# Output products on float16 parts scaled by row, and attention buffers in another order

## The chip, the cores and the metric

The kernel runs on one core of a Trainium2 chip. The time is the device time of one execution in microseconds (us). The engines are TensorE (PE, with its weight loads shown as PEld), VectorE (DVE), ScalarE (ACT), GpSimd (POOL) and SyncE (SP), which issues the DMA transfers. Each engine works through its own list of instructions in order; semaphores make it wait for the others.

## What is computed

Three parts follow each other: attention over 8 batches and 8 heads with 576 tokens of 64 values and a block-causal mask; a soft mixture of 8 experts with 4 slots each; and a feed-forward layer with a squared ReLU. Its weights `w_in` and `w_out` come as float64.

```python
def _attn_ref(q, k, v):                      # [8, 8, 576, 64] each
    ...
    scores = scale * np.matmul(q, k.transpose(0, 1, 3, 2))
    block_i = pos[:, None] // block
    block_j = pos[None, :] // block
    scores = np.where(block_i >= block_j, scores, -1000000000.0)
    scores = scores - np.max(scores, axis=-1, keepdims=True)
    attn = np.exp(scores)
    attn = attn / (np.sum(attn, axis=-1, keepdims=True) + 1e-09)
    return np.matmul(attn, v).astype(np.float32)

def _moe_ref(x, phi, w1, w2):                # x [4608, 512], phi [512, 32]
    logits = x @ phi
    d = np.exp(logits - logits.max(0, keepdims=True))
    d /= d.sum(0, keepdims=True) + 1e-09
    slot_input = (d.T @ x).reshape(E, S_per_e, D)
    for e in range(E):
        h = np.maximum(slot_input[e] @ w1[e], 0.0)
        slot_out[e] = h @ w2[e]
    ...
    c = np.exp(logits - logits.max(1, keepdims=True))
    c /= c.sum(1, keepdims=True) + 1e-09
    return (c @ slot_out).astype(np.float32)

def _moe2_ref(x, w_in, w_out, s, b):         # w_in [512, 2048], w_out [2048, 512]
    h = x @ w_in
    r = np.maximum(h, 0.0)
    g = s * (r * r) + b
    return (g @ w_out).astype(np.float32)
```

## The kernel before

The 4608 tokens are 36 tiles of 128. Attention runs as 32 pairs of heads whose operations are put in order by a planner from due times; in it the float16 products `pv` of probabilities and values (L405 to L407) take the probabilities and values as a high and a low part. Its buffers lie in the pools `earlyp` and `latep`. Weights come in as `wseq` lists them: four pairs of tiles of `w_in`, then eight tiles `wo_0` to `wo_7` of `w_out`, then 16 pieces of w1 and 16 of w2 (1 MB each, in two halves). Twelve tiles have a place from the start (`NPRE`); the four last of `w_out` go to the pool `wlate`, the expert weights to `NPOST` places of the pool `wpost` and to those that become empty (`advance`, `used`). These pools lie where attention's buffers were, so a load waits until the buffers under it are free. SP issues the loads in this order.

After attention comes the middle. A float64 value is turned into float32 by `from_f64` (L604 to L620): DVE cuts exponent (`cve`) and mantissa (`cvm`) out of the high word, ACT turns the low word into a float (`cvf`, L611) and shifts the exponent (L612), DVE puts the parts together (L614, L615), and `finish` follows, one function a step. For `w_out`, `split_wo` has three: the value (DVE, L690), its high part rounded to fp32r (ACT, L696) and its low part, the rest (DVE, L251), both into one tile `wo_is`. Two conversions run at a time; `convert` takes one step of each in turn, so the instructions of a pair of tiles alternate. Between them stand the expert products on PE: `expert1` (L787) into hp, then `hs` and `hTz` (L801 to L806), `expert2` (L815) into so, 32 pieces in all. The same rounds take up six chains `combine` (L760 to L777) for the combine weights: a maximum (DVE), a difference (POOL), an exponential (ACT, L767), sum and reciprocal (DVE), and the parts `cs` (POOL, ACT).

Then the slots stage: `slot_rows` copies so into `sos` (ACT, L861), transposes it (L864) and copies it to `soT` (DVE, L865). `slots` multiplies it by the converted `w_in` (L872, L879) into `mst`, 2048 columns, which holds a high part in its upper and a low part in its lower rows. `ctrans` transposes three token tiles of `cs` into `ct` (L626).

The output stage has 12 groups g of three token tiles, and in each 16 steps f of 128 rows of `w_out`. A step's h product is mst by ct (PE, L902, 384 columns), r its ReLU (ACT, L904), g is s·r² (DVE, L910), rh the rounded g + b (ACT, L916), rl the rest (DVE, L918). Four steps later (`LAG`) nine o products of 512 columns follow: for each token tile rh by high, rh by low and rl by high (L930 to L932). After 16 steps `stage_e` copies the three results and sends them out. All matrix operands here are fp32r. The order of this stage and of the middle is the order of the code.

## Time and profile before

| | us |
|---|---|
| three runs | 1007.74, 1008.96, 1010.03 |
| median | 1008.96 |
| the profiled execution | 1010.36 |
| its span in the profile | 1008.6 |

| engine | busy us | share of the span |
|---|---|---|
| PE | 902.7 | 89% |
| DVE | 696.9 | 69% |
| ACT | 564.7 | 56% |
| POOL | 283.7 | 28% |

The rows further down are of two views. A window row gives a stretch of the span, its length, for PE, PEld, DVE, ACT and POOL the busy time with the count of instructions, then the TensorE clock that was granted (1.00 is 2.4 GHz, 0.50 is 1.2 GHz), the share of the DMA engines that was busy and GB/s. A timeline row gives the start of an instruction, how long it is shown, engine, line, operation, out<-in with the partitions, shape and type; "x2" stands for so many alike in a row, and brackets for the idle time before it and what ended that. Matrix instructions overlap in the engine, so their pitch is the difference of two starts, not the duration shown.

### The profile page before, as it was taken

To read this page: it belongs to the slowest core of one execution; us is meant where nothing else is said; L and a number is where in the kernel's file an instruction comes from. 1 tells how busy PE (TensorE), PEld (TensorE's weight loads), DVE (VectorE), ACT (ScalarE), POOL (GpSimd) and SP (SyncE) were. 2 spreads that over 40 slices of the span, in tenths; PEclk is the share of its full clock that TensorE was granted. 3 is DMA by queue.
4 is the path that set the end of the run, shared out by engine and by line. 5 is a ranking of instruction groups with operands and counts; after the bars stand their busy time and mean duration, and the time that the engine had idled before them with its cause. 6 is when DMAs were issued, how large, how long until landed. Compare 5 with 4: busy or idle time off the path is not lost.

```text
span 1008.6 us, 20366 instructions
## 1 busy us (share of the span) xinstructions
PE 902.7 (89%) x8032; PEld 689.5 (68%) x8032; DVE 696.9 (69%) x1236; ACT 564.7 (56%) x974; POOL 283.7 (28%) x223
## 2 busy tenths in 40 slices
PE   3999989988999899955765999999999999999998
PEld 2777767766777777732111588888888888888886
DVE  5798979878989788768995555555555555555553
ACT  2677767767777677743453544444444444444442
POOL 6576647655666566720003000000000000000000
PEclk9999999989999999975978899999999999999999
DMA  4535445344434443085994000000000100010001
GB/s 113 129 85 121 121 104 130 79 106 119 111 98 123 104 101 101 4 333 203 403 385 176 1 1 32 32 26 8 32 32 1 31 32 1 32 32 6 26 32 31
DMA packets 150927, 91.73 MB, mean 91 GB/s; under 512 B 127472, under 2 KB 127792, under 8 KB 150832
## 3 DMA queue, kind: packets, MB, share of 16 engines
q1 hardware_dynamic: 150832, 90.44, 30.1%
q8 instruction: 63, 1.03, 0.4%
q14 instruction: 32, 0.26, 0.1%
HBM read 80.81 MB, written 9.44 MB: 89 GB/s over the span
## 4 chain that ended last, share of the span: by engine, by line
PE 60%; DVE 23%; ACT 7%; issue 3%; POOL 3%; DMA 2%; SPq 1%; DVEq 0%; ACTq 0%; POOLq 0%
PE o L932 13%; PE o L931 13%; PE o L930 13%; PE s L367 5%; DVE vl L345 3%; PE h L902 3%; DVE mm L281 3%; ACT pc L372 3%; PE tp L257 3%; DVE cvf L614 2%; DMA mr<-mT 2%; PE s L292 2%; DVE cve L615 2%; ACT ph L244 2%; PE pv L405 2%
## 5 line engine op out<-in xcount | busy, mean ns | idle before, releaser
L251 POOL TENSOR_TENSOR pl<-pc,ph 128x896 f16<-128x896 f32 (+1 forms) x128 | 232.2, 1815 | 153.3 <-ACT ph L244 79.3
L910 DVE SCALAR_TENSOR_TENSOR g<-r,s_sb 128x384 f32<-128x384 f32 x192 | 118.6, 618 | 156.9 <-ACT r L904 155.6
L904 ACT ACTIVATE r<-h 128x384 f32<-128x384 f32 x192 | 94.1, 491 | 197.8 <-PE h L902 197.8
L372 ACT ACTIVATE pc<-s 128x896 f32<-128x896 f32 (+1 forms) x128 | 110.6, 864 | 80.6 <-PE s L367 52.6
L918 DVE SCALAR_TENSOR_TENSOR rl<-g,b_sb,rh 128x384 fp32r<-128x384 f32 x192 | 117.7, 613 | 6.9 <-ACT rh L916 6.9
L916 ACT ACTIVATE rh<-g,b_sb 128x384 fp32r<-128x384 f32 x192 | 116.9, 609 | 0.6 <-DVE g L910 0.6
L244 ACT CAST ph<-pc 128x896 f16<-128x896 f32 (+1 forms) x128 | 113.4, 886 | 4.1
L281 DVE TENSOR_REDUCE mm<-s 128x2 f32<-128x1024 f32 (+3 forms) x128 | 101.8, 817 | 9.0 <-PE s L292 8.9
L405 PE MATMUL pv<-vh,ph 128*128 128x65 f16 x960 | 102.8, 196 | 1.7 <-DVE xt L421 1.5
L405 PEld LDWEIGHTS <-ph 128*128 128x128 f16 x960 | 86.8, 98 | 23.9 <-issue 6.7
L407 PE MATMUL pv<-vh,pl 128*128 128x65 f16 x960 | 101.3, 194 | 1.4 <-POOL pl L251 1.4
L406 PE MATMUL pv<-vl,ph 128*128 128x64 f16 x960 | 101.6, 193 | 0.0
L407 PEld LDWEIGHTS <-pl 128*128 128x128 f16 x960 | 88.9, 98 | 1.6 <-POOL pl L251 1.5
L406 PEld LDWEIGHTS <-ph 128*128 128x128 f16 x960 | 88.8, 99 | 0.0
L251 DVE TENSOR_TENSOR kql<-tp,kq 128x512 fp32r<-128x512 f32 (+1 forms) x96 | 57.5, 599 | 30.2 <-ACT kq L273 29.2
L257 PE MATMUL tp<-idF,rqk 128*128 128x128 f32 x320 | 58.5, 301 | 21.1 <-DVE kql L251 8.6
L367 PE MATMUL s<-mr,neg 64*128 64x128 f32 (+3 forms) x384 | 68.0, 321 | 7.4 <-DMA mr<-mT 7.0
L367 PE MATMUL s<-kq 64*128 64x128 f32 (+3 forms) x384 | 71.2, 367 | 0.7
L292 PE MATMUL s<-kq 64*128 64x64 f32 (+4 forms) x384 | 55.9, 337 | 16.8 <-DVE me L281 11.2
L902 PE MATMUL h<-ct,mst 128*128 128x384 f32 x192 | 65.5, 342 | 1.4 <-ACT r L904 1.4
L345 DVE SCALAR_TENSOR_TENSOR vl<-rv,al,vh 128x640 f16<-128x640 f32 x32 | 63.9, 1996 | 0.9 <-POOL vh L342 0.9
L273 ACT CAST kq<-tp 128x512 fp32r<-128x512 f32 (+1 forms) x96 | 48.5, 505 | 27.2 <-PE tp L257 27.0
(241 smaller groups left out, 2060.1 us busy)
## 6 DMA issues: line engine op xcount, KB each, us to landing
w2h<-in_moe_w_dram SPq DMA_DIRECT2D x34, 512.0 KB
w<-in_moe_w_dram SPq DMA_DIRECT2D x30, 512.0 KB
rqk<-in_k_dram SPq DMA_DIRECT2D x64, 128.0 KB
rqk<-in_q_dram SPq DMA_DIRECT2D x64, 128.0 KB
rv<-in_v_dram SPq DMA_DIRECT2D x64, 128.0 KB
wi<-in_moe_w_in_dram SPq DMA_DIRECT2D x8, 1024.0 KB
wo<-in_moe_w_out_dram SPq DMA_DIRECT2D x8, 1024.0 KB
out_dram<-ob SPq DMA_DIRECT2D x32, 256.0 KB
```

Source lines behind the costliest of these rows:

```text
L244: ACT.copy(o, i)
L251: eng.tensor_tensor(out=o, in0=i, in1=h, op=ALU.subtract)
L281: DVE.tensor_reduce(out=o, in_=i, axis=AX, op=ALU.max)
L367: PE.matmul(ps[:, h, o:o + c1 - c0], a[r], b[r], start=(n == 0), stop=(n == 3))
L372: ACT.activation(out=pc[:, :, 0:w], in_=st.pop(("ps", p, c))[:, :, 0:w], func=AF.Exp, scale=scale)
L405: PE.matmul(o, a, vh[:, 2 * sl + h, 0:65], start=(c == 0 and n == 0), stop=False)
L406: PE.matmul(o[:, 0:64], a, vl[:, 2 * sl + h, :], start=False, stop=False)
L407: PE.matmul(o, l, vh[:, 2 * sl + h, 0:65], start=False, stop=(c == 3 and n == len(UNIT[c]) - 1))
L910: DVE.scalar_tensor_tensor(out=g0, in0=r, scalar=s_sb, in1=r, op0=ALU.mult, op1=ALU.mult)
L930: PE.matmul(o, rh[:, 128 * i:128 * i + 128], hl[f][0], start=(f == 0), stop=False)
L931: PE.matmul(o, rh[:, 128 * i:128 * i + 128], hl[f][1], start=False, stop=False)
L932: PE.matmul(o, rl[:, 128 * i:128 * i + 128], hl[f][0], start=False, stop=(f == 15))
```

## The change

**Output products.** `rh`, `rl` and the two parts of `w_out` become float16. So that they keep to float16's range, each row of `w_out` (a partition and a half of a tile) is multiplied by a power of two: a new step `power` of `split_wo` stands between value and high. ACT sums the magnitudes of a row of 512 (`wsum`, with the accumulating output), DVE turns the sum's exponent into an inverse power (`wpow`), and ACT scales that by 2^13. High is then written by two scaled copies of 512 on ACT, low by two operations of 512 on DVE. Two tiles `wo` now share one home, so every second conversion frees a place for an expert weight. The g side takes the inverse: s and b become `sk` and `bk`, a column for each f, which follow from a bound over `mst`, s, b and `wsum`. That takes 16 transposes of mst, a maximum over them, some small operations on 128 x 16, a product on PE to bring the maximum over the partitions, and more small ones; they stand between the last `mst` and the first g. `stage_e` multiplies by `mu`, which undoes the scale.

**Buffers.** Attention's buffers are allocated in the order in which the last pairs of heads free them; `wlate` is opened ahead of `e1` and handed out from its other end; `cvm` has one buffer instead of two, and `NPOST` is 4.

```diff
@@ -18,7 +18,7 @@
 PSUM = bass.MemoryType.PSUM
 
 NPRE = 12
-NPOST = 3
+NPOST = 4
 
 SLOT = {
     "ld_k": -28.8, "ld_q": -28.6, "ld_v": -18.0,
@@ -121,6 +121,9 @@
     m896 = const.tile([128, 1], F32, name="m896")
+    eps = const.tile([128, 1], F32, name="eps")
+    wsum = const.tile([128, 16], F32, name="wsum")
+    wpow = const.tile([128, 16], F32, name="wpow")
@@ -137,6 +140,7 @@
     POOL.memset(m896, -896.0 * 2.0 ** 23)
+    POOL.memset(eps, 2.0 ** -100)
@@ -145,13 +149,18 @@
     RQK = [earlyp.tile([128, 2, 5, 128], F32, name=f"rqk_{i}") for i in range(2)]
-    RV = [earlyp.tile([128, 5, 128], F32, name=f"rv_{i}") for i in range(2)]
-
-    KQ = [earlyp.tile([128, 2, 640], F32R, name=f"kq_{i}") for i in range(3)]
-    KQL = [earlyp.tile([128, 2, 640], F32R, name=f"kql_{i}") for i in range(3)]
-
-    MR = [earlyp.tile([128, 640], F32R, name=f"mr_{i}") for i in range(2)]
+    KQ, KQL, MR = [None] * 3, [None] * 3, [None] * 2
+    for p in (NP - 3, NP - 2, NP - 1):
+        KQ[p % 3] = earlyp.tile([128, 2, 640], F32R, name=f"kq_{p % 3}")
+        KQL[p % 3] = earlyp.tile([128, 2, 640], F32R, name=f"kql_{p % 3}")
+        if p == NP - 3:
+            RV = [earlyp.tile([128, 5, 128], F32, name=f"rv_{i}") for i in range(2)]
+        else:
+            MR[p % 2] = earlyp.tile([128, 640], F32R, name=f"mr_{p % 2}")
@@ -602,7 +611,7 @@
-        m = pool.tile([128, n], I32, tag="cvm", name="cvm")
+        m = pool.tile([128, n], I32, tag="cvm", name="cvm", bufs=1)
         e = pool.tile([128, n], I32, tag="cve", name="cve")
         f = pool.tile([128, n], F32, tag="cvf", name="cvf")
@@ -642,8 +651,8 @@
+    wlate = wholes(ctx, "wlate", 16 - NPRE, reuse_waits="tile")
     e1 = later(ctx, "e1", 1)
-    wlate = wholes(ctx, "wlate", 16 - NPRE, reuse_waits="tile")
     P["cv"] = later(ph2, "cv", 2)
     wpost = places(ph2, "wpost", NPOST, reuse_waits="tile")
@@ -674,7 +683,7 @@
 
             key = toload.pop(0)
-            home[key] = wlate.pop() if key[0] == "wo" else empty.pop()
+            home[key] = wlate.pop(0) if key[0] == "wo" else empty.pop()
             load_w(key, home[key])
 
     def used(key):
@@ -686,22 +695,39 @@
     def split_wo(i):
         def value(u, s):
             DVE.tensor_tensor(out=u, in0=u, in1=s, op=ALU.mult)
 
+        def power(u, s):
+            for h in range(2):
+                ACT.activation(out=s[:, 512 * h:512 * h + 512], in_=u[:, 512 * h:512 * h + 512], func=AF.Abs, bias=eps,
+                               accum_out=wsum[:, 2 * i + h:2 * i + h + 1])
+            DVE.tensor_scalar(out=wpow[:, 2 * i:2 * i + 2].bitcast(I32), in0=wsum[:, 2 * i:2 * i + 2].bitcast(I32),
+                              scalar1=0x7F800000, scalar2=0x7F800000, op0=ALU.bitwise_and, op1=ALU.bitwise_xor)
+            ACT.mul(wpow[:, 2 * i:2 * i + 2], wpow[:, 2 * i:2 * i + 2], 2.0 ** 13)
         def high(u, s):
-            t = home["wo", i].tile([128, 2048], F32R, tag="w", name=f"wo_{i}s")
+            if i % 2 == 0:
+                st["wos", i // 2] = home["wo", i].tile([128, 2, 2, 2, 512], F16, tag="w", name=f"wo_{i}s")
+            t = st["wos", i // 2][:, i % 2]
             for h in range(2):
-                hl[2 * i + h] = t[:, 512 * h:512 * h + 512], t[:, 1024 + 512 * h:1536 + 512 * h]
-            ACT.copy(t[:, 0:1024], u)
-            st["wos", i] = t
+                hl[2 * i + h] = t[:, h, 0], t[:, h, 1]
+                ACT.activation(out=t[:, h, 0], in_=u[:, 512 * h:512 * h + 512], func=AF.Copy,
+                               scale=wpow[:, 2 * i + h:2 * i + h + 1])
 
         def low(u, s):
-            t = st.pop(("wos", i))
-            lo(DVE, t[:, 1024:2048], u, t[:, 0:1024].bitcast(F32))
+            for h in range(2):
+                DVE.scalar_tensor_tensor(out=hl[2 * i + h][1], in0=u[:, 512 * h:512 * h + 512],
+                                         scalar=wpow[:, 2 * i + h:2 * i + h + 1], in1=hl[2 * i + h][0],
+                                         op0=ALU.mult, op1=ALU.subtract)
             ready.update((2 * i, 2 * i + 1))
-
-        return from_f64(wt["wo", i], P["cv"], [value, high, low])
+            if i % 2:
+                empty.append(split(home["wo", i], i))
+                advance()
+        return from_f64(wt["wo", i], P["cv"], [value, power, high, low])
 
     def conv_in(i):
 
@@ -882,6 +908,9 @@
+        sb_abs = e1.tile([128, 2], F32, name="sb_abs")
+        ACT.activation(out=sb_abs[:, 0:1], in_=s_sb, func=AF.Abs)
+        ACT.activation(out=sb_abs[:, 1:2], in_=b_sb, func=AF.Abs)
         slot_rows()
         ctrans(0, pm, "n")
         gens = [slots(i) for i in range(8)]
@@ -890,6 +919,34 @@
                 next(gens[i])
             if i >= 2:
                 next(gens[i - 2], None)
+        mt = pm.tile([128, 512], F32, tag="m", name="m")
+        for f in range(16):
+            PE.transpose(mt[:, 32 * f:32 * f + 32].bitcast(F32R), mst[0:32, 128 * f:128 * f + 128], idR[0:32, 0:32])
+        def small(name, n=16):
+            return e1.tile([128, n], F32, name=name)
+        mm, bound, gpow, sk, bk, rs_, mu = (small(n) for n in ("mmax", "bound", "gpow", "sk", "bk", "rscale", "mu"))
+        DVE.tensor_reduce(out=mm, in_=mt.rearrange("p (f n) -> p f n", n=32), axis=AX, op=ALU.max)
+        DVE.tensor_tensor(out=mm, in0=mm, in1=mm, op=ALU.mult)
+        DVE.tensor_scalar(out=mm, in0=mm, scalar1=sb_abs[:, 0:1], scalar2=sb_abs[:, 1:2], op0=ALU.mult, op1=ALU.add)
+        DVE.tensor_scalar(out=gpow.bitcast(I32), in0=wsum.bitcast(I32), scalar1=0x7F800000, scalar2=None, op0=ALU.bitwise_and)
+        DVE.tensor_tensor(out=bound, in0=mm, in1=gpow, op=ALU.mult)
+        DVE.tensor_reduce(out=mu[:, 0:1], in_=bound, axis=AX, op=ALU.max)
+        gp = pm.tile([128, 512], F32, tag="n", name="n")
+        PE.matmul(gp[:, 0:128], mu[:, 0:1].to_broadcast([128, 128]), idF, start=True, stop=True)
+        DVE.tensor_reduce(out=mu[:, 1:2], in_=gp[:, 0:128], axis=AX, op=ALU.max)
+        DVE.tensor_scalar(out=mu[:, 1:2], in0=mu[:, 1:2], scalar1=2.0 ** -60, scalar2=None, op0=ALU.max)
+        DVE.tensor_scalar(out=mu[:, 2:3].bitcast(I32), in0=mu[:, 1:2].bitcast(I32), scalar1=0x7F800000, scalar2=0x7F800000,
+                          op0=ALU.bitwise_and, op1=ALU.bitwise_xor)
+        DVE.tensor_scalar(out=rs_, in0=gpow, scalar1=mu[:, 2:3], scalar2=2.0 ** 13, op0=ALU.mult, op1=ALU.mult)
+        DVE.tensor_scalar(out=sk, in0=rs_, scalar1=s_sb, scalar2=1.0, op0=ALU.mult, op1=ALU.mult)
+        DVE.tensor_scalar(out=bk, in0=rs_, scalar1=b_sb, scalar2=1.0, op0=ALU.mult, op1=ALU.mult)
+        DVE.tensor_scalar(out=mu[:, 3:4].bitcast(I32), in0=mu[:, 1:2].bitcast(I32), scalar1=0x7F800000, scalar2=None,
+                          op0=ALU.bitwise_and)
+        DVE.tensor_scalar(out=mu[:, 3:4], in0=mu[:, 3:4], scalar1=2.0 ** -28, scalar2=None, op0=ALU.mult)
     ph3.close()
@@ -907,15 +964,15 @@
         def stage_g(g, f):
             r = rr_[g, f]
             g0 = e3.tile([128, 384], F32, tag="g0", name="g0")
-            DVE.scalar_tensor_tensor(out=g0, in0=r, scalar=s_sb, in1=r, op0=ALU.mult, op1=ALU.mult)
+            DVE.scalar_tensor_tensor(out=g0, in0=r, scalar=sk[:, f:f + 1], in1=r, op0=ALU.mult, op1=ALU.mult)
             rr_[g, f] = g0
 
         def stage_r(g, f):
             g0 = rr_[g, f]
-            rh = e4.tile([128, 384], F32R, tag="rh", name="rh")
-            ACT.activation(out=rh, in_=g0, func=AF.Identity, bias=b_sb)
-            rl = e4.tile([128, 384], F32R, tag="rl", name="rl")
-            DVE.scalar_tensor_tensor(out=rl, in0=g0, scalar=b_sb, in1=rh.bitcast(F32), op0=ALU.add, op1=ALU.subtract)
+            rh = e4.tile([128, 384], F16, tag="rh", name="rh")
+            ACT.activation(out=rh, in_=g0, func=AF.Identity, bias=bk[:, f:f + 1])
+            rl = e4.tile([128, 384], F16, tag="rl", name="rl")
+            DVE.scalar_tensor_tensor(out=rl, in0=g0, scalar=bk[:, f:f + 1], in1=rh, op0=ALU.add, op1=ALU.subtract)
             rr_[g, f] = (rh, rl)
 
         ops = {}
@@ -935,9 +992,9 @@
             for i in range(3):
                 ob = e3.tile([128, 512], F32, tag="ob", name="ob")
                 if i == 1:
-                    DVE.tensor_copy(ob, ops[g][i])
+                    DVE.tensor_scalar(out=ob, in0=ops[g][i], scalar1=mu[:, 3:4], scalar2=1.0, op0=ALU.mult, op1=ALU.mult)
                 else:
-                    ACT.copy(ob, ops[g][i])
+                    ACT.activation(out=ob, in_=ops[g][i], func=AF.Copy, scale=mu[:, 3:4])
                 for p0, p1, r0 in tok_rows(3 * g + i):
                     SP.dma_start(out=out[r0:r0 + p1 - p0, :], in_=ob[p0:p1, :])
 
```

DVE in the conversion of the second pair of `w_out` tiles, from the second tile's first instruction on; before:

```order
L608 TENSOR_SCALAR cve<-wo_7680 128x1024
L609 TENSOR_SCALAR cvm<-wo_7680 128x1024
L614 SCALAR_TENSOR_TENSOR cvf<-cvm,cvf 128x1024
L615 SCALAR_TENSOR_TENSOR cve<-wo_7680,cve 128x1024
L690 TENSOR_TENSOR cvf<-cvf,cve 128x1024
L251 TENSOR_TENSOR wo_2s<-cvf,wo_2s 128x1024
L251 TENSOR_TENSOR wo_3s<-cvf,wo_3s 128x1024
```

and after:

```order
L617 TENSOR_SCALAR cve<-wo_7684 128x1024
L618 TENSOR_SCALAR cvm<-wo_7684 128x1024
L707 TENSOR_SCALAR wpow<-wsum 128x2
L623 SCALAR_TENSOR_TENSOR cvf<-cvm,cvf 128x1024
L624 SCALAR_TENSOR_TENSOR cve<-wo_7684,cve 128x1024
L700 TENSOR_TENSOR cvf<-cvf,cve 128x1024
L707 TENSOR_SCALAR wpow<-wsum 128x2
L722 SCALAR_TENSOR_TENSOR wo_2s<-cvf,wpow,wo_2s 128x512 x4
```

An operation on `wpow`, which reads ACT's sums, now stands ahead of the second tile's L623 and another behind its value; low comes in halves.

ACT from the last exponentials of combine (c) to the slot copies; before, where the same two rows stand twice more ahead of these:

```order
L767 ACTIVATE c<-c 128x192 x2
L244 CAST cs<-c 128x6x32 x2
L861 COPY sos<-so 128x512
L628 CAST ct<-n 64x384
L876 COPY part<-m 128x256 x2
L881 CAST mst<-n 128x256 x2
L876 COPY part<-m 128x256
L881 CAST mst<-n 128x256 x2
```

and after, from the first exponentials on:

```order
L793 ACTIVATE c<-c 128x192 x2
L887 COPY sos<-so 128x512
L253 CAST cs<-c 128x6x32 x2
L637 CAST ct<-n 64x384
L902 COPY part<-m 128x256
L793 ACTIVATE c<-c 128x192 x2
L902 COPY part<-m 128x256
L907 CAST mst<-n 128x256
L253 CAST cs<-c 128x6x32
L907 CAST mst<-n 128x256
L902 COPY part<-m 128x256
L253 CAST cs<-c 128x6x32
```

`sos` stood behind all six chains; now it stands behind the first two exponentials, and the other chains alternate with part and mst.

PE at the start of the output stage; before:

```order
L879 MATMUL n<-part,J_8831 128x256 x3
L902 MATMUL h<-ct,mst 128x384 x5
L930 MATMUL o_9470<-wo_0s,rh 128x512
L931 MATMUL o_9470<-wo_0s,rh 128x512
L932 MATMUL o_9470<-wo_0s,rl 128x512
```

and after:

```order
L905 MATMUL n<-part,J_8845 128x256 x3
L926 MATMUL m<-idR,mst 128x32 x16
L939 MATMUL n<-idF,mu 128x128
L959 MATMUL h<-ct,mst 128x384 x5
L987 LDWEIGHTS rh
L987 MATMUL o_9570<-wo_0s,rh 128x512
L988 LDWEIGHTS rh
L988 MATMUL o_9570<-wo_0s,rh 128x512
L989 LDWEIGHTS rl
```

The transposes of mst (L926) and the product that spreads the maximum (L939) come between the last slot product and the first h, and each o product has a weight load ahead of it.

## Rows read from the trace of the kernel before

**Rows 1.** Windows: length, then busy time (count) per engine, granted clock, DMA share.
```profile
486.00:537.00 51.00, 34.79 (x159) 7.20 (x158) 48.13 (x51) 25.61 (x26) 0.00 (x0) 0.87 1.04 390
...
551.00:566.00 15.00, 13.73 (x93) 6.87 (x93) 5.92 (x14) 6.03 (x17) 0.59 (x1) 0.75 0.00 1
...
566.00:572.00 6.00, 5.05 (x14) 3.83 (x15) 4.98 (x10) 3.94 (x9) 0.00 (x0) 0.73 0.00 0
...
572.00:1004.00 432.00, 432.00 (x1938) 356.82 (x1936) 228.51 (x398) 202.95 (x409) 0.00 (x0) 1.00 0.06 21
```

**Rows 2.** Timeline of PE in the output stage: start, duration, engine, line, operands.
```profile
573.96 0.34 PE L902 MATMUL h<-ct,mst 128*128 128x384 f32 x1
...
576.23 0.34 PE L902 MATMUL h<-ct,mst 128*128 128x384 f32 x1
...
703.37 0.33 PE L902 MATMUL h<-ct,mst 128*128 128x384 f32 x1
...
703.54 0.39 PE L930 MATMUL o<-wo_5s,rh 128*128 128x512 f32 x1
...
705.61 0.33 PE L902 MATMUL h<-ct,mst 128*128 128x384 f32 x1
```

**Rows 3.** The end of attention: one window, then PE's timeline.
```profile
430.00:435.00 5.00, 3.62 (x83) 3.13 (x81) 0.69 (x1) 2.04 (x4) 4.55 (x4) 1.00 0.48 166
...
432.30 0.20 PE L405 MATMUL pv<-vh,ph 128*128 128x65 f16 x1
...
432.90 0.19 PE L407 MATMUL pv<-vh,pl 128*128 128x65 f16 x1
```

**Rows 4.** Timeline of DVE during the conversion of w_out.
```profile
486.04 0.69 DVE L608 TENSOR_SCALAR cve<-wo 128x1024 int32<-128x1024 int32 x1
...
491.57 0.69 DVE L609 TENSOR_SCALAR cvm<-wo 128x1024 int32<-128x1024 int32 x1
...
495.89 1.22 DVE L251 TENSOR_TENSOR wo_0s<-cvf,wo_0s 128x1024 fp32r<-128x1024 f32 x1
...
498.29 0.69 DVE L608 TENSOR_SCALAR cve<-wo 128x1024 int32<-128x1024 int32 x1
...
513.58 1.23 DVE L614 SCALAR_TENSOR_TENSOR cvf<-cvm,cvf 128x1024 f32<-128x1024 int32 x1 [1.75 <-ACT cvf L611]
```

**Rows 5.** Timeline of ACT: one Square of attention, then the conversion.
```profile
401.43 0.73 ACT L325 ACTIVATE sq<-rv 128x640 bf16<-128x640 f32 x1
...
491.69 1.15 ACT L612 ACTIVATE cve<-cve,m 128x1024 int32<-128x1024 int32 x1 [2.74 <-DVE cve L608]
...
509.27 0.68 ACT L801 ACTIVATE hs<-hp,rs 128x512 f32<-128x512 f32 x1
...
512.07 0.45 ACT L806 ACTIVATE hTz<-htp 128x128 f32<-128x128 f32 x2 [2.12 <-PE htp L804]
```

**Rows 6.** Timelines of DVE, ACT and PE from conversion's end to the first g.
```profile
536.68 0.60 DVE L763 TENSOR_REDUCE mc<-lgs 128x6 f32<-128x192 f32 x2
...
537.64 0.83 ACT L767 ACTIVATE c<-c 128x192 f32<-128x192 f32 x2 [2.14 <-POOL c L765]
...
538.43 0.17 DVE L771 TENSOR_SCALAR sc<-sc 128x6 f32<-128x6 f32 x1
...
543.75 1.05 PE L815 MATMUL so<-w2h,hTz 128*32 128x512 f32 x4 [0.23 <-DMA w2h<-in_moe_w_dram]
...
551.09 0.58 ACT L861 COPY sos<-so 128x512 f32<-128x512 f32 x1
...
553.45 0.51 PE L626 MATMUL n<-idR,cs 128*64 128x128 f32 x3
...
566.07 1.15 DVE L910 SCALAR_TENSOR_TENSOR g<-r,s_sb 128x384 f32<-128x384 f32 x2
```

**Rows 7.** One window before the experts, and the first expert product on PE.
```profile
455.00:460.00 5.00, 0.72 (x2) 0.36 (x2) 4.82 (x10) 2.29 (x2) 1.34 (x1) 0.50 0.00 0
...
465.30 4.97 PE L787 MATMUL hp<-w,slotT 128*32 128x512 f32 x24 [0.45 <-DVE slotT L750]
```

## The prediction

> **What bounds the kernel now.** I read the busy time by stretch first, then the timeline of single instructions at the seams. From 572 to 1004 us TensorE (PE) is busy without a gap at full granted clock, while VectorE (DVE) and ScalarE (ACT) work about half the time [rows 1]. In this output stage 192 steps of nine o matmuls and one h matmul follow each other, and the time is PE's pitch. The step is 576.23 − 573.96 = 2.27 us early and 705.61 − 703.37 = 2.24 late, on average 2.255; one h takes 703.54 − 703.37 = 0.17, so an o takes (2.255 − 0.17) / 9 = 231.7 ns [rows 2]. At 2.4 GHz 512 columns at one a cycle would be 213.3, so 18 ns of each o is excess.
>
> Before it, from 486 to 537, DVE converts w_out and is the bound (48.1 of 51 us busy; PE has 34.8) [rows 1]. Then the combine weights hold ACT until it copies the slot outputs (`sos`, 551.09), and the slot products follow until the first g at 566.07 [rows 6]. So the seconds that count are two: PE's pitch after 572, and whatever starts the output stage later than now.
>
> **The change part by part.**
>
> *Float16 in the output products.* 9 × 192 = 1728 o matmuls keep their count and columns; their operands become float16, with a weight load of its own. The trace has float16 products on this engine: the pv matmuls of attention, 64 or 65 columns (mean 64.67), each with its own weight load. From 432.30 to 432.90 there are 20 intervals, 30 ns each, at granted clock 1.00 [rows 3]. 64.67 columns are 26.9 ns at 2.4 GHz, an excess of 3 ns, weight load included. I take a fixed excess: 213.3 + 3 = 216.3 ns. Bounds: no excess, 213.3; and the excess of fp32r as it is, 231.7. I take the float16 row since it is the operands' own type, though at fewer columns. Step: 9 × 0.2163 + 0.17 = 2.117, a saving of 0.138 × 192 = **26.5 us** (bounds 0 and (231.7 − 213.3) × 1728 = 31.8). DVE and ACT need 228.5 and 203.0 us of these 432 [rows 1]; with the same operations per step at the same sizes neither becomes the bound. The rescaling by `mu` is done by the copies that already move o to `ob`.
>
> The Trainium skill, page "TensorE: Matmul & The Clock Gate", section "Wait — 56ns, not 53.3ns?", gives 215.7 ns for back-to-back warm matmuls of 512 columns; by it the sum would be 9 × 0.2157 + 0.17 = 2.111, or 27.6 us saved, and the 3 ns of the rows agree with its 2.5.
>
> *Conversion of w_out.* Now a pair of tiles takes DVE 498.29 − 486.04 = 12.25 us without a stop, and the four pairs end at 536.68 [rows 4, 6]. The change puts into each tile, between value and high, two Abs sums of 512 on ACT, a small DVE operation (`wpow`) on their result and a small ACT one. DVE's order is unchanged otherwise, so DVE stands in front of `wpow`. First tile: DVE is done with the second tile's masks at 491.57 + 0.69, 6.2 after the start of the pair; ACT starts that tile's Relu at 491.69, 5.65 after, and is done at 6.8 [rows 4, 5]; only then come the two Abs. An Abs with a sum is priced by sq (640 columns, 0.73) [rows 5], for 512 about 0.6; so ACT ends at 8.0 and DVE has stood 1.8. Second tile: value ends where now low begins, 9.9 after the start [rows 4], plus 1.8 is 11.7; two Abs and the hand-over make 13.1: DVE stands 1.3. The two small operations cost 0.3 by the 0.17 of sc [rows 6], and 0.15 goes to waiting for the last high. In all 3.55 a pair, 14.2 for four. Low is cut in halves of the same columns, nothing by itself. Bounds: 2 a pair if ACT gets the Abs in ahead of that Relu, 5.5 if ACT is another 2 late, as the 1.75 at 513.58 shows it can be [rows 4]; 8 to 22.
>
> In the second pair ACT also has `hs` and the Relu copies, 509.27 to 512.4, which now hold up DVE by 1.75 at 513.58 [rows 4, 5]. They come to stand between the mul and the high of wo_3, and DVE's stop becomes about 2.85: +1.1. So conversion ends at 536.68 + 15.3 = 552.0.
>
> *Who waits for that.* Now `sos` stands on ACT behind all three pairs of combine chains, 551.09 − 536.68 = 14.4 after conversion [rows 6]. In the new order it stands behind the first pair's two exponentials only, which end at 537.64 + 0.83, or 1.8 after. So `sos` comes at 553.8, not 551.09 + 15.3: a gain of **12.6**. PE's last so (543.75 + 1.05) is long done by then [rows 6]. The other combine work is now interleaved with the slot copies on ACT and DVE. Its exponentials, casts and reductions are short, and in 551 to 566 both engines are 60% idle [rows 1]; but a slot copy that stands behind a chain waits for POOL. I take +1.3, a few such waits; bounds 0 and two pairs of 14.4 / 3 = 4.8 each in series, 9.6.
>
> *The bound chain.* Between the last mst and the first g now stand, in series: 16 transposes of 32 columns, of which only the last counts (0.1), a maximum over 512 columns (0.65: 0.17 for 6 columns, as above, and 1 ns for each more, by g's 0.57 for 384 [rows 6]), five small dependent operations (1.0), a PE product and a maximum over it (0.9: 0.5 for three such on PE [rows 6], and 0.3), and some six small ones until `sk`, `bk` (1.2); together 3.9, with hand-overs **4.1**. Bounds 3 (half of the small ones hidden) and 6 (a PE leg of 2.1, as `htp` takes [rows 5]). The h matmuls stand on PE behind the chain's product, but DVE's g waits longer than they do. Clock: it is 0.73 from 566 to 572 [rows 1], and PE now idles before it; +0.5, bounds 0 and 6 × 0.27 = 1.6.
>
> *Buffers.* Attention's buffers in the order they come free, and the late w_out tiles first, let loads start earlier. Nothing waits for them: from 455 to 460 DMA has no work at all, and the first expert product starts at 465.30 with 0.45 idle behind slotT on DVE, not behind a load [rows 7]. The fourth place for w1/w2 likewise helps a stream that ends 8 us before conversion does. I cost all this at 0; its cover is DVE's conversion, and the most it could bring is 2.9, all that DVE idles from 486 to 537 [rows 1].
>
> *Sum.* The output stage starts later by 14.2 + 1.1 − 12.6 + 1.3 + 4.1 + 0.5 = **8.6 us** (4 to 15) and is 26.5 shorter: −17.9. The profiled execution took 1010.36 us (span 1008.6 and 1.76 around it): 992.5. It is 1.40 above the median of the three runs, so the forecast is 991.0.
>
> **Rivals.**
>
> *A, slower: float16 products of 512 columns go no faster than fp32r.* If the 18 ns lie in the array or the accumulator and not in reading the operands, the pitch stays 231.7 and only the delay is left: 1008.96 + 8.6 = 1017.6. It decides at 8.6 / 1728 = 5.0 ns: with a pitch above 226.7 the kernel is slower. For: float16 shows at 65 columns only, and fp32r too has a small excess at few columns. Against: the same instruction has 2.27 us a step with one set of w_out tiles and 2.24 with another [rows 2], so the excess depends on where operands are read, and halving their bytes should matter. Chance 0.10.
>
> *B, the preparation is much longer.* Combine fully in series with the slots (+8) and DVE standing 5.5 a pair (+8): delay 25, net −1.5, 1007.5, no change. For: ACT and DVE run in order, and each chain passes ACT, POOL and DVE. Against: 60% idle there. Chance 0.05.
>
> *C, the preparation is nearly hidden.* DVE stands 2 a pair, and combine and the clock cost nothing: delay 0 to 4, 982 to 986. Chance 0.08.
>
> *D, products overlap further.* If a next product could start before the last has streamed its columns, with its weights already loaded, PE would cease to bound the stage and DVE's 228.5 us would [rows 1]: 432 − 228.5 = 203.5 less, about 814 with the delay. No matmul of rows 2 or 3 goes below one column a cycle. Chance 0.01. The Trainium skill's same page, section "Back-to-back issue gap", gives 131 ns as the sustained pitch for a stream of weight loads and 512-column products; by that (231.7 − 131) × 1728 = 174 us would go, and the rows, 30 ns for 65 columns, speak against it.
>
> That the change doesn't do what it says holds for the buffers alone: loads go earlier and no one is waiting.
>
> **How the numbers follow.** Forecast 0.76, A 0.10, B 0.05, C 0.08, D 0.01. The forecast's own range is 984 (no excess, delay 7) to 998 (delay 15). The range to hold 8 in 10 goes on to no excess with a delay of 4 or less below, and to a pitch of 221 with a delay of 12 above: 980 to 1003; A, most of B and D stay out. A measurement of this kernel can tell about 0.2%, 2 us, from no change. Faster: 0.76 + 0.08 + 0.01 = 0.85; B falls within (0.04) or just beyond (0.01); slower 0.10 + 0.01 = 0.11.
>
> **What would show it.** Right: two h matmuls in mid-stage 2.11 to 2.13 us apart; DVE idle 1 to 2 us before each `wpow`, with ACT's Abs as releaser; conversion ending near 552; `sos` about 2 us behind it; the first g near 575 instead of 566. Wrong: steps still above 2.2 (A); `sos` after 560 or gaps of several us between slot products (B); conversion before 542 (C); PE waiting for a w2 load after conversion's end, which would make the buffers count.

## The result and the profile after

| | before | after |
|---|---|---|
| median of four runs, us | 1009.17 | 996.18 |
| lowest and highest, us | 1007.74, 1010.03 | 995.61, 997.07 |
| profiled execution and its span, us | 1010.36, 1008.6 | 996.41, 994.7 |

The ratio is 0.9873, with an interval of 0.9856 to 0.9891: 13 us less. That lies within the stated range of 980 to 1003 and 5 us above the forecast of 991.0.

The windows of the changed kernel, with the columns of [rows 1]; those behind the conversion are set some 8 us later, since the output stage starts later:

```profile
486.00:537.00 51.00, 29.43 (x158) 7.05 (x158) 36.94 (x49) 31.59 (x57) 0.00 (x0) 0.77 0.95 366
...
552.00:570.00 18.00, 13.88 (x101) 7.15 (x101) 11.83 (x40) 8.58 (x26) 9.06 (x18) 0.75 0.00 1
...
570.00:580.00 10.00, 6.86 (x24) 3.62 (x24) 8.16 (x24) 4.31 (x9) 0.35 (x1) 0.55 0.01 2
...
580.00:990.00 410.00, 409.98 (x1942) 191.11 (x1939) 228.16 (x398) 205.02 (x409) 0.00 (x0) 1.00 0.06 22
```

DVE works 36.9 us of the 51 us from 486 to 537, which now lie wholly within the conversion of w_out; it had 48.1 [rows 1]. The rest of the time it stands still. In the output stage PE is busy without a gap at full clock as before.

PE's timeline in the output stage (L959 is the h product, L987 to L989 are the o products):

```profile
701.44 0.39 PE L987 MATMUL o<-wo_4s,rh 128*128 128x512 f16 x1
...
701.67 0.38 PE L988 MATMUL o<-wo_4s,rh 128*128 128x512 f16 x1
...
703.18 0.38 PE L989 MATMUL o<-wo_4s,rl 128*128 128x512 f16 x1
...
703.21 0.52 PE L959 MATMUL h<-ct,mst 128*128 128x384 f32 x1
...
703.57 0.39 PE L987 MATMUL o<-wo_4s,rh 128*128 128x512 f16 x1
```

From 701.67 to 703.18 there are seven o products, 216 ns each, where [rows 2] gave 231.7. From one first o to the next, 703.57 − 701.44, is a step of 2.13 us; nine times 0.216 leaves 0.187 for the h product and the change to it and back, where [rows 2] had 0.17.

The next row is the eighth h product, from which on the steps have their full pitch; [rows 2] has it at 576.23 in the kernel before:

```profile
585.07 0.52 PE L959 MATMUL h<-ct,mst 128*128 128x384 f32 x1
```

DVE's timeline from the first conversion of w_out to the first g:

```profile
484.85 0.69 DVE L617 TENSOR_SCALAR cve<-wo 128x1024 int32<-128x1024 int32 x1
...
493.09 0.17 DVE L707 TENSOR_SCALAR wpow<-wsum 128x2 int32<-128x2 int32 x1 [2.02 <-ACT cve L704]
...
498.36 0.17 DVE L707 TENSOR_SCALAR wpow<-wsum 128x2 int32<-128x2 int32 x1 [1.58 <-ACT cve L704]
...
501.09 0.68 DVE L617 TENSOR_SCALAR cve<-wo 128x1024 int32<-128x1024 int32 x1
...
518.79 1.42 DVE L722 SCALAR_TENSOR_TENSOR wo_2s<-cvf,wpow,wo_2s 128x512 f16<-128x512 f32 x2 [2.70 <-ACT wo_2s L717]
...
552.63 0.60 DVE L789 TENSOR_REDUCE mc<-lgs 128x6 f32<-128x192 f32 x2
...
574.65 0.61 DVE L967 SCALAR_TENSOR_TENSOR g<-r,sk 128x384 f32<-128x384 f32 x1
```

Compare [rows 4]: the first pair takes 501.09 − 484.85 = 16.24 us instead of 12.25. In brackets stands why: 2.02 and 1.58 us in front of the two `wpow` (L707), behind ACT's Abs (L704). The 2.70 at 518.79 is `hs` and its copies, ahead of the high part on ACT. Conversion ends at 552.63 (the first maximum of combine), and the first g comes at 574.65 instead of 566.07 [rows 6].

ACT's timeline at the same places:

```profile
490.50 1.15 ACT L621 ACTIVATE cve<-cve,m 128x1024 int32<-128x1024 int32 x1 [2.73 <-DVE cve L617]
...
491.56 0.71 ACT L704 ACTIVATE cve<-cvf,eps 128x512 f32<-128x512 f32 x1
...
492.17 0.18 ACT L704 ACTIVATION_READ_ACCUMULATOR cve<-cvf,eps 128x1 f32 x1
...
554.33 0.57 ACT L887 COPY sos<-so 128x512 f32<-128x512 f32 x1
```

The Relu of the second tile runs from 490.50, and only behind it the first Abs starts. An Abs takes 0.61 until its read-out and 0.70 until the next one. `sos` comes at 554.33, 1.70 behind the conversion.

That the conversion starts 1.2 us earlier (484.85 against 486.04) is not the change's doing. The last products of attention, before and then after:

```profile
435.06 0.19 PE L407 MATMUL pv<-vh,pl 128*128 128x65 f16 x1
...
433.80 0.19 PE L416 MATMUL pv<-vh,pl 128*128 128x65 f16 x1
```

Attention itself ended 1.26 us earlier. Over the profiled executions of all kernels here it ends between 432.0 and 437.4, with the same products and with either order of the buffers. It ends the later, the longer the granted clock was 0.50 before: 6.8 us in those that end by 433.6, 13.7 in the kernel before, 10.2 in the changed one, 23.9 in the latest. From its last product to the first conversion of w_out it is 51.0 us in both kernels.

### The profile page after: what moved, and what is told of

Same layout as the page of the kernel before. It is cut to its first block, busy times and chain, and to the rows that moved or that the text cites. A ratio compares the mean times of both kernels' runs of the same rounds, so it can differ in the third digit from the quotient of the medians.

```text
span 994.7 us, 20474 instructions
## 1 busy us (share of the span) xinstructions
PE 873.4 (88%) x8050; PEld 522.2 (52%) x8050; DVE 701.5 (71%) x1266; ACT 581.7 (58%) x1024; POOL 284.3 (29%) x224
## 4 chain that ended last, share of the span: by engine, by line
PE 58%; DVE 25%; ACT 9%; issue 3%; POOL 2%; DMA 2%; SPq 1%; DVEq 0%; POOLq 0%; ACTq 0%
PE o L987 13%; PE o L989 13%; PE o L988 13%; PE s L376 5%; DVE vl L354 5%; DVE mm L290 3%; ACT pc L381 3%; PE h L959 3%; PE tp L266 2%; ACT ph L253 2%; DVE cvf L623 2%; DVE cve L624 2%; PE s L301 2%; DMA mr<-mT 2%; PE pv L414 1%
## 5 line engine op out<-in xcount | busy, mean ns | idle before, releaser
L967 DVE SCALAR_TENSOR_TENSOR g<-r,sk 128x384 f32<-128x384 f32 x192 | 118.5, 617 | 138.6 <-ACT r L961 138.2
L975 DVE SCALAR_TENSOR_TENSOR rl<-g,bk,rh 128x384 f16<-128x384 f32 x192 | 117.4, 612 | 6.8 <-ACT rh L973 6.7
L973 ACT ACTIVATE rh<-g,bk 128x384 f16<-128x384 f32 x192 | 116.3, 606 | 1.0 <-DVE g L967 1.0
L959 PE MATMUL h<-ct,mst 128*128 128x384 f32 x192 | 99.3, 519 | 1.3 <-ACT r L961 1.3
L987 PEld LDWEIGHTS <-rh 128*128 128x128 f16 x576 | 56.1, 97 | 82.4 <-issue 35.8
L989 PEld LDWEIGHTS <-rl 128*128 128x128 f16 x576 | 56.5, 98 | 68.6 <-issue 0.8
L988 PEld LDWEIGHTS <-rh 128*128 128x128 f16 x576 | 56.7, 98 | 46.1 <-issue 0.6
```

Of the source, the lines that this page charges most:

```text
L959: PE.matmul(hps, mst[:, 128 * f:128 * f + 128], ct[g], start=True, stop=True)
L987: PE.matmul(o, rh[:, 128 * i:128 * i + 128], hl[f][0], start=(f == 0), stop=False)
L988: PE.matmul(o, rh[:, 128 * i:128 * i + 128], hl[f][1], start=False, stop=False)
L989: PE.matmul(o, rl[:, 128 * i:128 * i + 128], hl[f][0], start=False, stop=(f == 15))
```

## The experiments

**The two parts apart.** `e1_buf` is the kernel before with the buffers of the change:

```diff
-NPOST = 3
+NPOST = 4
...
+    for p in (NP - 3, NP - 2, NP - 1):
+        KQ[p % 3] = earlyp.tile([128, 2, 640], F32R, name=f"kq_{p % 3}")
+        KQL[p % 3] = earlyp.tile([128, 2, 640], F32R, name=f"kql_{p % 3}")
...
-        m = pool.tile([128, n], I32, tag="cvm", name="cvm")
+        m = pool.tile([128, n], I32, tag="cvm", name="cvm", bufs=1)
...
+    wlate = wholes(ctx, "wlate", 16 - NPRE, reuse_waits="tile")
     e1 = later(ctx, "e1", 1)
-    wlate = wholes(ctx, "wlate", 16 - NPRE, reuse_waits="tile")
...
-            home[key] = wlate.pop() if key[0] == "wo" else empty.pop()
+            home[key] = wlate.pop(0) if key[0] == "wo" else empty.pop()
```

> The kernel before with the buffer part of the change alone (attention's buffers in the order they come free, the late w_out tiles first, one cvm buffer, four places). My theory, by the prediction: loads go earlier and nobody waits for them, so the time stays at 1009 within 2 us; at most the 1.2 us by which the first conversion of w_out started earlier in the changed kernel (484.85 against 486.04) may show: 1008. The output stage's pitch stays 231 ns. The rival, that the earlier loads carry a good part of the measured 13 us, expects 1004 or less.

Measured: 1012.92 against 1009.89, ratio 1.0032 (1.0014 to 1.0049): not faster, but 0.3% slower, which no theory had said. The last product of attention, PE's timeline in the second half of a group's steps, and DVE's first g:

```profile
433.41 0.19 PE L409 MATMUL pv<-vh,pl 128*128 128x65 f16 x1
...
699.82 0.34 PE L904 MATMUL h<-ct,mst 128*128 128x384 f32 x1
...
700.00 0.40 PE L932 MATMUL o<-wo_5s,rh 128*128 128x512 f32 x1
...
702.09 0.34 PE L904 MATMUL h<-ct,mst 128*128 128x384 f32 x1
...
564.04 1.15 DVE L912 SCALAR_TENSOR_TENSOR g<-r,s_sb 128x384 f32<-128x384 f32 x2
```

The first g comes 2.0 us earlier than in [rows 6], but 1.65 of that is attention, whose last product started at 433.41 in this execution and at 435.06 in the one of [rows 6]. From there to the first g it is 130.6 us against 131.0: the buffers bring 0.4. The step with `wo_5s` takes 702.09 − 699.82 = 2.27 us, where the same step had 2.24 in [rows 2]. The tiles `wo_4` to `wo_7` have another home now, and half of the 192 steps have become 27 ns longer: 96 x 0.027 = 2.6 us, which is most of the 3.0 by which the medians differ. The fp32r product's excess goes with where its operands lie; the products, their order and their columns are the same in both kernels. Which operand's place it is, and why, no run tells.

`e2_f16const` is the kernel before with float16 products alone:

```diff
-            t = home["wo", i].tile([128, 2048], F32R, tag="w", name=f"wo_{i}s")
+            t = home["wo", i].tile([128, 4096], F16, tag="w", name=f"wo_{i}s")
...
-            ACT.copy(t[:, 0:1024], u)
+            ACT.activation(out=t[:, 0:1024], in_=u, func=AF.Copy, scale=2.0 ** 12)
...
-            lo(DVE, t[:, 1024:2048], u, t[:, 0:1024].bitcast(F32))
+            DVE.scalar_tensor_tensor(out=t[:, 1024:2048], in0=u, scalar=2.0 ** 12, in1=t[:, 0:1024],
+                                     op0=ALU.mult, op1=ALU.subtract)
...
+        ACT.mul(sk, s_sb, 2.0 ** 9)
+        ACT.mul(bk, b_sb, 2.0 ** 9)
...
-            rh = e4.tile([128, 384], F32R, tag="rh", name="rh")
+            rh = e4.tile([128, 384], F16, tag="rh", name="rh")
```

> The kernel before with float16 output products alone: the powers of two are constants written into the kernel (2^12 for w_out, 2^9 for g), which leaves out the search for powers and bounds; buffers as before. My theory: the conversion takes 12.25 us a pair as before, the first g comes at 566 to 567, and the output stage goes by the pitch of the changed kernel, 2.131 us a step without the token transposes: 1009.2 - 0.123 x 192 = 985.6. If the buffers or the new order gave part of the saving, more than 990; if a saving in the stage is really owed to something else in the changed kernel, 1000 or more.

Measured: 986.52, ratio 0.9772 (0.9746 to 0.9799), 23 us less. DVE's timeline at the end of the conversion and at the first g:

```profile
537.30 0.61 DVE L766 TENSOR_REDUCE mc<-lgs 128x6 f32<-128x192 f32 x2
...
566.42 1.15 DVE L915 SCALAR_TENSOR_TENSOR g<-r,sk 128x384 f32<-128x384 f32 x2
```

Both are within 0.7 us of [rows 6] (536.68 and 566.07). So the float16 operands alone give 23 us, in the output stage. All else that the change does, the earlier `sos` included, costs 996.2 − 986.5 = 9.7 us.

`e3_nobuf` is the changed kernel with the edits of `e1_buf` undone.

> The changed kernel with the buffer part undone. My theory: the conversion starts 1.2 us later and sos stands behind two pairs of exponentials instead of one (4.8 us more), of which up to 4 come back since less of combine is left among the slot copies: 998 to 1002. The rival, that the buffer part is worth nothing in any form, expects 996 within 1 us.

Measured: 998.55, ratio 0.9893 (0.9868 to 0.9918); the changed kernel has 996.18, and its slowest run lies below the fastest of this one (997.07 and 997.94), though the two intervals overlap. DVE's first maximum of combine, then ACT's exponentials (L791) and `sos` (L885):

```profile
551.72 0.60 DVE L787 TENSOR_REDUCE mc<-lgs 128x6 f32<-128x192 f32 x2
...
552.69 0.83 ACT L791 ACTIVATE c<-c 128x192 f32<-128x192 f32 x2 [1.92 <-POOL c L789]
...
557.59 0.83 ACT L791 ACTIVATE c<-c 128x192 f32<-128x192 f32 x2 [1.17 <-POOL c L789]
...
558.32 0.57 ACT L885 COPY sos<-so 128x512 f32<-128x512 f32 x1
```

The conversion ends no later than with the buffers (551.72 against 552.63), and it takes as long, 67.8 us from its start, so nobody had waited for those loads. But `sos` stands behind a second pair of exponentials, 6.6 us after the conversion instead of 1.7. The code has the same order in both. Between the two blocks of the program, the middle and the slots, a scheduler places the instructions of the second among those of the first, and with the other buffers it places `sos` later. Of the 4.9 some comes back: from `sos` to the first g, at 577.47, are 19.2 us instead of 20.3, with less of combine left among the slot copies.

**What the preparation costs.** `e4_nochain` drops the bound chain:

```diff
-        mt = pm.tile([128, 512], F32, tag="m", name="m")
...
-        DVE.tensor_reduce(out=mu[:, 1:2], in_=gp[:, 0:128], axis=AX, op=ALU.max)
...
-        DVE.tensor_scalar(out=rs_, in0=gpow, scalar1=mu[:, 2:3], scalar2=2.0 ** 13, op0=ALU.mult, op1=ALU.mult)
+        DVE.tensor_scalar(out=rs_, in0=gpow, scalar1=2.0 ** -7, scalar2=2.0 ** 13, op0=ALU.mult, op1=ALU.mult)
```

> The changed kernel without the bound chain ahead of the output stage: the scale of g follows from the row powers of w_out and a constant, known early; the search for the largest mst and its spreading over the partitions are left out. My theory: the first g comes where the last mst ends, 4.2 us earlier, and the time falls from 996.2 to 992. A rival: PE's clock, low behind the idle time, costs the same wherever PE waits, and the stage starts with h products of its own; then the gain is under 3 us. If the chain had been hidden, 996.

Measured: 993.19, ratio 0.9834 (0.9809 to 0.9858). ACT's `sos`, then DVE's last mst (L908) and first g (L947), and PE's eighth h:

```profile
552.93 0.57 ACT L887 COPY sos<-so 128x512 f32<-128x512 f32 x1
...
568.69 0.43 DVE L908 TENSOR_TENSOR mst<-n,mst 64x256 fp32r<-64x256 f32 x1 [0.62 <-ACT mst L907]
...
569.15 1.15 DVE L947 SCALAR_TENSOR_TENSOR g<-r,sk 128x384 f32<-128x384 f32 x2
...
580.08 0.53 PE L939 MATMUL h<-ct,mst 128*128 128x384 f32 x1
```

The first g follows the last mst at once, and from `sos` to it are 16.2 us where the changed kernel has 574.65 − 554.33 = 20.3: the chain delays the first g by 4.1 us and nothing hides it. Part of the rival holds too: from the first g to the eighth h, where the steps have their full pitch, it takes 580.08 − 569.15 = 10.9 us here and 585.07 − 574.65 = 10.4 with the chain, so that 3.6 of the 4.1 are left. The medians differ by 3.0, and the intervals of the two ratios touch; the length of the chain is read from the trace and not from them.

`e7_beside` takes up the combine chains while the conversions run:

```diff
-            if combs and done["w1"] >= 4 and len(active) < CMOST:
-                active.append(combs.pop(0))
+            if done["w1"] >= 4:
+                pump(chains)
+                if combs and not chains:
+                    chains.append(combs.pop(0))
...
```

> The changed kernel with the combine chains beside the conversions from the fourth expert piece on, nothing else. My theory: their DVE and ACT work, some 2 us a chain, falls mostly into DVE's waits for wpow, conversion ends at 552 to 556, sos follows without the 1.7 us for the first exponentials, and the slot products lose the 1.1 us that interleaving cost: 994 to 997, no change that can be told. The rival, that combine among the slot copies is what costs (more than the 1.1 us), expects 990 or less; the other, that the chains delay ACT's Abs and with it every wpow, 1000 or more.

Measured: 996.13, ratio 0.9873 (0.9854 to 0.9892): no change from the changed kernel. DVE's waits in front of the two `wpow` of the last pair:

```profile
549.52 0.17 DVE L707 TENSOR_SCALAR wpow<-wsum 128x2 int32<-128x2 int32 x1 [2.27 <-ACT cve L704]
...
554.79 0.17 DVE L707 TENSOR_SCALAR wpow<-wsum 128x2 int32<-128x2 int32 x1 [0.89 <-ACT cve L704]
```

The second wait has shrunk from 1.6 to 0.89, since a chain's reductions fill it; the first has grown from 2.02 to 2.27, since ACT does a chain's exponential too. The conversion ends at 558.85, later than expected, since DVE now does the chains' work in between; `sos` doesn't wait for that end and comes at 554.67. From it to the first g, at 574.14, are 19.5 us, 0.8 less than in the changed kernel. So what interleaving costs looks small, as the prediction had it (1.3); the conversion's last parts, which now fall behind `sos`, may cover some of it.

`e8_sos` is the kernel before with one copy issued from another place:

```diff
         while todo or active or combs:
+            if len(ready) == 16 and "sos" not in st:
+                st["sos"] = e1.tile([128, 512], F32, tag="a1", name="sos")
+                ACT.copy(st["sos"], so)
             convert(CMOST)
...
-            sos = e1.tile([128, 512], F32, tag="a1", name="sos")
-            ACT.copy(sos, so)
+            sos = st["sos"]
```

> The kernel before with one instruction issued from another place: the copy sos directly behind the last conversion, so that the scheduler puts it behind the third chain's exponential and lets the other chains alternate with the slot copies. My theory, the prediction's term for sos: it then waits for the last so alone (543.75 + 1.05) and comes at 545 instead of 551.1; about 1.1 is lost in interleaving: 1004 to 1005. The rival, that the slot products are held by the chains left over and the early copy gains nothing, expects 1008 or more.

Measured: 1000.92 against 1009.5, ratio 0.9919 (0.9895 to 0.9943): 8.6 us less, more than the 5 expected. ACT, PE (the transposes of `sos` and the first 24 slot products) and DVE (the first g) in this kernel, and a window:

```profile
546.21 0.58 ACT L834 COPY sos<-so 128x512 f32<-128x512 f32 x1 [1.26 <-PE so L815]
...
546.85 1.08 PE L866 MATMUL m<-I,sos 128*128 128x32 f32 x8 [0.69 <-ACT sos L834]
...
548.31 1.50 PE L874 MATMUL m<-wi,soT 128*32 128x256 f32 x24 [0.20 <-DVE soT L867]
...
558.61 1.15 DVE L912 SCALAR_TENSOR_TENSOR g<-r,s_sb 128x384 f32<-128x384 f32 x2
...
552.00:558.00 6.00, 5.94 (x46) 2.71 (x38) 4.57 (x13) 3.50 (x12) 2.17 (x4) 1.00 0.00 0
```

and the same products and window of the kernel before:

```profile
551.72 1.92 PE L864 MATMUL m<-I,sos 128*128 128x32 f32 x8 [6.91 <-ACT sos L861]
...
554.02 2.79 PE L872 MATMUL m<-wi,soT 128*32 128x256 f32 x24
...
552.00:558.00 6.00, 5.93 (x41) 3.31 (x45) 1.27 (x3) 1.22 (x4) 0.00 (x0) 0.50 0.01 3
```

`sos` waits for the last so alone, as expected, and comes 4.9 us earlier. The first g comes 7.5 earlier, as 2.6 more are gained behind `sos`. (Attention ended 2.2 us later in this execution, its last product starting at 437.24 and not 435.06; counted from there, `sos` gains 7.1 us and the first g 9.6.) Most of the 2.6 is the clock: here PE comes from the so products with a pause of 0.69 us and has 1.00 in this stretch; in the kernel before it has had nothing for 6.91 us since the last so ended at 544.8 [rows 6] and has 0.50, the lower level of 1.2 GHz. The transposes take 1.08 us instead of 1.92 and the 24 products 1.50 instead of 2.79, which is 2.1 of the 2.6. So the early `sos`, which the change brings along by the scheduler, was to be had in the kernel before, for 8.6 us, without any float16.

**Where the step's last 14 ns went.** The step was forecast at 2.117 us and is 2.131. `e5_h16` puts h into float16 too:

```diff
-    mst = later(ctx, "mstp", 1).tile([128, 2048], F32R, name="mst")
+    mst = later(ctx, "mstp", 1).tile([128, 2048], F16, name="mst")
...
-        t = ct[g] = P["cpl"].tile([128, 384], F32R, tag="ct", name="ct")
+        t = ct[g] = P["cpl"].tile([128, 384], F16, tag="ct", name="ct")
```

> The changed kernel with the h product in float16 too: the combine weights (cs, ct) and mst as float16 high and low parts, the same columns and count. Unlike the o products they have no scale of their own. In the changed kernel a step is 2.131 us, nine o at 216 ns and 187 ns left for h, where 384 columns at 2.4 GHz are 160. Theory one: the 27 ns come from fp32r and from changing between it and float16; then h takes about 163 and the first o behind it loses nothing: step 2.107, 192 x 0.024 = 4.6 us less, 991.6. Theory two: they belong to any h, which brings other weights and another output between the o products; then the step stays within 4 ns and the time at 995.5 to 996.

Measured: 991.93, ratio 0.9835 (0.9812 to 0.9859), 4.25 less than the changed kernel. PE's timeline:

```profile
702.30 0.33 PE L961 MATMUL h<-ct,mst 128*128 128x384 f16 x1
...
702.46 0.38 PE L989 MATMUL o<-wo_4s,rh 128*128 128x512 f16 x1
...
704.40 0.33 PE L961 MATMUL h<-ct,mst 128*128 128x384 f16 x1
```

The step is 704.40 − 702.30 = 2.10 us, and h takes 702.46 − 702.30 = 0.16, its columns and no more. So the 0.187 of the changed kernel came from an fp32r product among float16 ones: theory one. Not every step gains: the two around the end of a group take 0.11 us longer, so that from the eighth h to the end of the span this kernel needs 3.2 us less than the changed one and not 4.6.

**Taking the waits away.** `e6_deep` opens three conversions at a time, with combine beside them as in `e7_beside`:

```diff
-NPOST = 4
+NPOST = 3
...
-    P["cv"] = later(ph2, "cv", 2)
+    P["cv"] = later(ph2, "cv", 3)
...
-    CMOST = 2
+    CMOST = 3
...
-        return from_f64(wt["wo", i], P["cv"], [value, power, high, low])
+        return from_f64(wt["wo", i], P["cv"], [value, sums, power, high, low])
```

> The changed kernel with three conversions at a time instead of two (a third cve and cvf buffer, in exchange for the fourth place of w1 and w2), the Abs sums a step of their own ahead of wpow, and one combine chain beside the conversions. The operations are the same. My theory: DVE stood still for 3.6 us a pair because only two conversions were open; now the next tile's work fills that, a pair takes about 12.6 us, and with some 7 us of combine the conversion ends near 542 instead of 552.6; sos then waits for the last so near 543, and the slot products are free of combine: 996.2 - 11 - 1 = 984. Rivals: ACT, whose work in a pair adds up to 10.4 us, comes too late anyhow and conversion ends after 548 (990 or more); or the w2 loads with three places become the bound (so ends after 546, 988 or more).

Measured: 991.96, ratio 0.984 (0.9812 to 0.9869), 8 us above the theory. PE's timeline (L814 is the last hp, L831 the transposes of hs, L842 the last so), ACT's `sos` and a window:

```profile
497.33 1.06 PE L814 MATMUL hp<-w2h,slotT 128*32 128x512 f32 x6 [0.20 <-DMA w2h<-in_moe_w_dram]
...
523.89 1.97 PE L831 MATMUL htp<-I,hs 128*128 128x64 f32 x8 [25.50 <-ACT hs L828]
...
553.63 1.05 PE L842 MATMUL so<-w,hTz 128*32 128x512 f32 x4 [0.22 <-DMA w<-in_moe_w_dram]
...
554.73 0.58 ACT L891 COPY sos<-so 128x512 f32<-128x512 f32 x1 [4.73 <-PE so L842]
...
514.00:524.00 10.00, 0.11 (x1) 0.11 (x1) 9.19 (x16) 7.18 (x17) 1.59 (x3) 0.50 0.31 119
```

hp was done at 498.4, but `hs` now stood on ACT behind more conversions, and PE waited 25.50 us for it. The so products, which need `hs`, could not free places for the w2 loads in that time: in the 10 us from 514 the DMA engines are busy 0.31 of the time, where [rows 1] has 1.04. The conversion ended at 546.83, but the last so came at 553.63 behind its load, and `sos` waited 4.73 us for it. A wait on DVE was taken away, and a wait on a load stood in its place; the rival's bound, by another way than it named.

`e9_all` and `e10_all2` move `hs` forward and take in `e5_h16`; `e9_all` has

```diff
-            for _ in range(CSUB):
+            if kind == "w2" or i % 2 == 0:
                 convert(CMOST)
```

and `e10_all2` has `i < 9` in place of `i % 2 == 0`.

> The run with three conversions at a time (e6_deep), with two things more: h in float16 as in e5_h16, and during the 16 products of w1 a round of conversion only behind every second one, so that ACT comes to hs when hp is ready and not behind later conversions. In e6_deep hs came at 523 though hp was done at 498, the w2 loads had no free place from 503 to 525, and the last so came at 554, where sos had to wait for it. My theory: with hs near 500 the loads flow, the last so ends before 543, conversion ends at 543 to 547 and sets sos; the output stage starts 8 to 11 us earlier than in e6_deep, and h gives the 4.6 us of e5_h16: 992 - 9 - 4.5 = 978. The rival, that the w2 stream itself, with three places, is the bound wherever hs stands: sos stays at 552 to 554 and the time at 987.

> As e9_all, but with a round of conversion behind each of the first nine w1 products and behind none of the others, which puts hs behind two more ACT steps of conversion. My theory: hs a little later than in e9_all, the loads a little later, conversion ends at the same place: within 2 us of e9_all, 977 to 980. If the place of hs decides by itself, 3 us or more above it.

Measured: 988.13, ratio 0.9791 (0.9768 to 0.9815), and 987.51, ratio 0.9784 (0.9755 to 0.9814). They stand within 1 us of each other, but some 10 above the theory. PE's last so, DVE and ACT in `e9_all` (L725 is the low part, L720 the high part):

```profile
539.83 1.05 PE L844 MATMUL so<-w2h,hTz 128*32 128x512 f32 x4 [0.21 <-DMA w2h<-in_moe_w_dram]
...
509.54 1.41 DVE L725 SCALAR_TENSOR_TENSOR wo_0s<-cvf,wpow,wo_0s 128x512 f16<-128x512 f32 x2 [4.47 <-ACT wo_0s L720]
...
551.08 2.87 DVE L725 SCALAR_TENSOR_TENSOR wo_6s<-cvf,wpow,wo_6s 128x512 f16<-128x512 f32 x4 [0.45 <-ACT wo_6s L720]
...
553.02 0.56 ACT L893 COPY sos<-so 128x512 f32<-128x512 f32 x1
```

The loads flow now and the last so starts at 539.83, but the conversion ends at 553.95, as late as in the changed kernel: the high parts stand on ACT behind `hs` and its copies, and DVE idles 4.47 us at 509.54 for them. Its waits from 487 to 554 add up to 8.2 us, where the theory counted on next to none. In `e6_deep` `hs` waited, here the high parts do. An order that serves both was not found. These two, which can't be told apart, are the fastest of the kernels here that compute everything: some 21 us below the kernel before and 8 to 9 below the changed one.

## Why the prediction held, and where it was off

Each step against the profiled executions:

| term | forecast | measured | from |
|---|---|---|---|
| start of the conversion | 0 | −1.2 | 484.85 against 486.04; attention's end, not the change |
| conversion of w_out | +15.3 | +17.1 | 552.63 − 484.85 against 536.68 − 486.04 |
| `sos` behind conversion | −12.6 | −12.7 | 1.70 against 14.4 |
| `sos` to first g, interleaving and chain | +5.4 | +5.3 | 20.3 against 15.0 |
| clock at the start, first steps | +0.5 | +0.3 | the eighth h, 585.07 against 576.23, less the rows above |
| output stage from there on | −26.5 | −22.8 | to the end of the span: 994.68 − 585.07 against 1008.65 − 576.23 |
| sum | −17.9 | −14.0 | 996.41 − 1010.36 |

*The o products.* The main term rested on 20 intervals of 65-column products [rows 3] and gave 216.3 ns; measured are 216. Rival A's 231.7 is out. `e1_buf` fits the argument against it, that the fp32r excess depends on where operands are read: it moves with their place, and float16 products have 2.13 us a step with either set of tiles. Why the excess is there no run shows. The Trainium skill, page "TensorE: Matmul & The Clock Gate", section "Wait — 56ns, not 53.3ns?", gives 215.7 ns; the trace agrees, with 216. The 131 ns of its section "Back-to-back issue gap" don't appear: a stream of 512-column products, each with its own weight load, stays at 216.

*The term that was mis-sized* is h. The prediction left h at 0.17 because it is not changed; among float16 products it takes 0.187, which over 192 steps is 3.3 us: 1728 x 15.7 ns for o less that is 23.8, where 26.5 were forecast. The measured row, −22.8, leaves out the first steps, which lie in the row above. `e5_h16` shows that it is the mixture. No row of the kernel before had the two types side by side, so this cost needed bounds and got none.

*Conversion.* This is the second term that was too small. DVE stood 2.02 and 1.58 a pair where 1.8 and 1.3 were forecast, as an Abs takes 0.70 and not 0.6. That attention happened to end 1.26 us earlier in the profiled execution hid most of the difference: luck. The pair with `hs` has 2.70 in place of 1.75, forecast 2.85.

*Buffers.* Nobody waits for the loads: that held (`e1_buf`, `e3_nobuf`). But "costed at 0" was wrong twice. In the kernel before they move the fp32r operands and cost 2.6 us of pitch; in the changed kernel they change the scheduler's place for `sos` and bring 2.4 by the medians. The earlier start of the conversion is not theirs.

*The level.* The forecast took 1.40 us off the profiled time, since that lay above the median of before. The changed kernel's profiled run lies 0.2 above its median; 1.2 of the 5 us are that.

B is out by the 20.3 us from `sos` to g and the waits of 2.02 and 1.58, C by the 17.1 us of conversion, D by the 216 ns. The −12.7 for `sos` is read from the trace. `e8_sos` shows in the kernel before that the place of `sos` sets the start of the output stage, and that it has nothing to do with float16; how much of the 12.7 an early `sos` is worth in the changed kernel was not measured by itself. What is open: why the fp32r excess goes with the operands' place, and whether conversion and w2 stream can both be served, which `e6_deep` to `e10_all2` did not reach.

## What to carry to other kernels

Price a changed operand type from the nearest instructions of that type in the same trace, even if they are far smaller, but give the neighbours that keep the old type a price too: here an fp32r product among float16 ones cost 17 ns more than among its own kind. Where a scheduler merges two blocks, read its order around the seam before and after; a copy that lands ahead of a chain was worth 8.6 us here, a third of what float16 brings, and can be had without it. Compare two profiles from a point that the edit cannot touch: here the first 432 to 437 us differ from execution to execution, by more than some of the effects. Opening more conversions brought 4 of the 12 us hoped for and moved the wait to what stood behind them on ACT.
